# Two fill products between a step's row scores and its key scores: a fused attention and Fourier kernel on one Trainium2 core

## The chip, the cores and the metric

The kernel runs on one core of a Trainium2 chip. The core has five engines with their own queues: TensorE for matrix products (PE; PEld is its loading of the stationary operand), VectorE (DVE), ScalarE (ACT), GpSimd (POOL) and SyncE (SP), whose queue issues almost all DMAs. The metric is the time of one execution in microseconds, measured on the device. Three executions of the kernel before took 2702.86, 2702.91 and 2704.59 us (median 2702.91).

## The reference

Two independent layers are computed in float32, and their results are laid side by side:

```python
# A: attention, 32 heads of width 32 that share one key head and one value head; S = 2048, D = 1024
q = (x @ wq).reshape(B, S, H, Dh).transpose(0, 2, 1, 3)
k = x @ wk
v = x @ wv
p = softmax(einsum("bhqd,bkd->bhqk", q, k) * Dh ** -0.5)
a = einsum("bhqk,bkd->bhqd", p, v).transpose(0, 2, 1, 3).reshape(B, S, D) @ wo
# B: real part of a two-dimensional Fourier transform as matrix products
y = dft_seq_re @ (x @ dft_hid_re.T) - dft_seq_im @ (x @ dft_hid_im.T)
out = concatenate([a, y], axis=-1)
```

## The kernel before

**Products.** Each float32 product of 128x512 is made of three products of split operands (`rh`, `rl` of the right side, `mh`, `ml` of the left side, a high and a low part each), and they accumulate in one of two PSUM banks named `psb`. These products, for the query projection, the Fourier layer and the output projection, are called **fill products** here. They stand in one long list of groups of 12 or 24 products. `take(n)` issues the next n of them and, when a group ends, its copy or addition out of `psb` on DVE; `pump` issues the loads and splits that later products need.

**Attention.** The attention runs as a loop of 1024 steps, 32 units of 32 steps. A unit is 512 query rows of four heads. In step n the loop issues, in this order on PE:

- a pair of products into a `pss` tile: scores with the query rows on the partitions, 128 rows by 1024 keys (`scores`). DVE takes the row maximum into `nm` (TENSOR_REDUCE), and ACT later forms exp(score - maximum) and its row sum (ACTIVATE and ACTIVATION_READ_ACCUMULATOR on `pss`). These are the **row scores**, and they run 44 steps ahead of the key scores. `score_step(s)` issues the pair of score s, then on ACT the row sum of score s-1. There are two `pss` tiles, so the pair of score s waits for the row sum of score s-2.
- a pair of products into the `pst` tile: scores with the keys on the partitions, 128 keys by 1024 query columns, with the log of the row's sum already folded in (`expo`). ACT turns them into probabilities `p`. These are the **key scores**. There is only one `pst` tile, so the pair of step n waits for the exponential of step n-1.
- at three steps of each unit (r = 0, 12 and 22, `ENDS`), called **block ends** here: a block of products of `p` with the values `v` (`pv`), which may first finish a few fill products (`aside`).
- at every other step: some fill products, `level(n)`. It spreads the remaining list evenly up to the next block end, and comes out at 4 to 7 a step. The step ahead of a block end holds five fill products at 91 of the 95 block ends that have a block of values (6 or 7 at the others), by the program's own order.

At r = 16 `inverse` issues four DMAs that fetch the inverse row sums (`rb`). In the last 44 steps no row scores are left, and a step is a key-score pair and six or seven fill products.

All engines keep the order in which the program was written (`keep_in_program_order`), so an instruction that waits on PE holds up everything behind it there. Every instruction stands under line 79 in the profile, the one that keeps this order, so groups are told apart by tile.

Of the kernel before, what the change touches and what calls it, by code (L numbers as in the profile page):

```python
# [101 lines left out]
def tile_kernel(ctx: ExitStack, tc, xT, wq, wkv, wo, xbT, wT, cT, out):  # L102
# [51 lines left out]
    class Line:  # L154
# [24 lines left out]
        def pump(self):  # L179
            for k in range(4):  # L180
                while self.may(k) and self.items[self.n[k]].due - self.lead[k] <= pos["fill"]:
                    self.step(k)
# [94 lines left out]
    def add(gs):  # L277

        for g in gs:
            i0 = g.at = end[0]  # L280
            end[0] += g.n
            if groups and g.set[0] is not groups[-1].set[0]:
                prev["set"] = prev["this"]
                prev["this"] = i0
            for c, it in enumerate(g.right):
                if it.need is None:
                    it.need = i0 + 3 * c
                    p0 = min(prev["set"], i0 - it.back)
                    it.due = min(it.need, p0 + (i0 - p0) * (g.first + c + 1) // (len(g.set) * len(g.right))) - it.ahead
                    RL.items.append(it)  # L290
                it.last = i0 + 3 * c + 2
            for c, it in enumerate(g.left):
                if it.need is None:
                    it.need = it.due = i0 + 12 * c
                    ML.items.append(it)
                it.last = i0 + 12 * c + 11
            for it in g.ys:
                it.due = i0 + g.n
                ylist.append(it)
            groups.append(g)  # L300
# [14 lines left out]
    def at(p, f):  # L315
        k = len(later)
        while k and later[k - 1][0] > p:
            k -= 1
        later.insert(k, (p, f))

    def run_later():
        while later and later[0][0] <= pos["fill"]:
            later.pop(0)[1]()
# [29 lines left out]
    def bank(name, open_=False):  # L353

        while held:
            held.pop(0)()
        b = 1 - cur["bank"] if cur["bank"] is not None else int(used[1] < used[0])
        cur["at"] += 1
        used[b] = cur["at"]
        if open_:  # L360
            cur["bank"] = b
        return ps_b[b].tile([P, W], F32, name=name)
# [10 lines left out]
    def product(g, ps, j):  # L373
        c, w = divmod(j, 3)
        l, r = g.left[c // 4], g.right[c]
        a = (l.lo if w == 2 else l.hi)[:, c % 4]
        te.matmul(ps[:g.rows], a, r.lo if w == 1 else r.hi, start=j == 0, stop=j == g.n - 1)

    def take(n):
        for _ in range(n):  # L380
            if cur["group"] >= len(groups):
                return
            g = groups[cur["group"]]
            j = pos["fill"] - g.at
            if j == 0:
                cur["ps"] = bank("psb", True)
            if j % 3 == 0:
                RL.force(g.right[j // 3])
            if j % 12 == 0:
                ML.force(g.left[j // 12])  # L390
            product(g, cur["ps"], j)
            pos["fill"] += 1
            if j == g.n - 1:
                cur["group"] += 1
                assert all(hasattr(it, "done") for it in g.ys)
                g.post(cur["ps"])
                cur["at"] += 1
                used[cur["bank"]] = cur["at"]
                cur["bank"] = None
                if g.ys:  # L400
                    at(pos["fill"] + 2 * BEHIND + 5, lambda n=len(g.ys): yused.__setitem__(0, yused[0] + n))
            pump()
            run_later()
# [174 lines left out]
    def wo_set(e):  # L578
        return [Item([(lambda g=g: wo[g * P:(g + 1) * P, e * W:(e + 1) * W], 1)]) for g in range(NG)]
# [90 lines left out]
    def o_group(b, t, e, ws):  # L670
        def post(ps):
            r0 = b * W + t * P
            to = out[r0:r0 + P, e * W:(e + 1) * W]
            if b < NQ - 1:
                oo = op.tile([P, W], F32, name="qh")
                dve.tensor_copy(oo, ps)
                store(to, oo)
                return

            n = len(halves)  # L680
            halves.append(n)
            oo = pp.tile([P, 2, W], F32, name="p")
            if n + 1 < 8:
                if n % 2:
                    dve.tensor_copy(oo[:, 0], ps)
                else:
                    act.activation(oo[:, 0], ps, AF.Copy)
                move(act, to, oo[:, 0])
                return
            for k, q in enumerate((act, sp)):  # L690
                cols = slice(k * W // 2, (k + 1) * W // 2)
                if k:
                    dve.tensor_copy(oo[:, k, :W // 2], ps[:, cols])
                else:
                    act.activation(oo[:, k, :W // 2], ps[:, cols], AF.Copy)
                move(q, to[:, cols], oo[:, k, :W // 2])
        return Group([o_left(b, t, q) for q in range(2)], ws, post)
# [101 lines left out]
    def inverse(u):  # L799
        rb[u] = onp.tile([P, W], F32, name="rb")  # L800
        for h in range(4):
            r = r_d[u][4 * h:4 * h + 4].rearrange("t c -> (t c)")
            sp.dma_start(rb[u][h * DH:(h + 1) * DH], r.unsqueeze(0).to_broadcast([DH, W]))

    def expo(n):
        u, r = divmod(n, SU)
        c, hp_ = divmod(r, 2)
        pt[u, c, hp_] = pp.tile([P, 2, W], F32, name="p")
        ps = ps_t.tile([P, 2, W], F32, name="pst")
        for a in range(2):  # L810
            te.matmul(ps[:, a], kst[:, c * P:(c + 1) * P], qst[u][:, 2 * hp_ + a], start=True, stop=True)
        act.activation(pt[u, c, hp_], ps, AF.Exp)
# [45 lines left out]
    def score_step(s):  # L858

        if s < total:  # L860
            u, r = divmod(s, SU)
            if r == SU - 6 and u + 1 < len(units):
                open_unit(u + 1)
        if SU <= s < SU * (len(units) + 1) and s % SU == TURN:
            row_sums(s - 1)
            lse_3((s - SU) // SU)
        if s < total:
            scores(s)
        row_sums(s - 1)
        u, e = divmod(s - SU, SU)  # L870
        if 0 <= u < len(units):
            for f in LSE.get(e, ()):
                f(u)
# [52 lines left out]
    def goal(n):  # L926
        return PRO + (FILL - PRO - LAST - MORE * (total - QUIET)) * n // total + MORE * max(n - QUIET, 0)
# [4 lines left out]
    def level(n):  # L932
        r = n % SU
        if r in ENDS:
            return
        more = min(e for e in ENDS if e > r) - r
        left = goal(n + more) - pos["fill"]
        take(round(left / more))

    for n in range(total):  # L940
        u, r = divmod(n, SU)
        if n == total - 12:
            w1 = wo_set(1)
            add([o_group(NQ - 1, t, e, ws) for e, ws in ((0, w0), (1, w1)) for t in range(4)])
        score_step(n + SU + LEAD)
        if ends:
            ends.pop(0)()
        expo(n)
        if r == 16:
            inverse(u)  # L950
        if r in ENDS and n:
            pv((n - 1) // SU, (ENDS.index(r) - 1) % (len(CUT) - 1))
        level(n)


    last = groups[len(groups) - 8:]
# [75 lines left out]
```

## Time and profile before

| what | value |
|---|---|
| median of three executions | 2702.91 us |
| profiled execution's own time | 2701.05 us |
| its span, first to last instruction | 2699.3 us |
| ACT busy | 2134.8 us (79%) |
| POOL busy | 1723.7 us (64%) |
| DVE busy | 1592.8 us (59%) |
| row maximum on DVE (TENSOR_REDUCE `nm<-pss`) | 1024 of 1223 ns |
| exponential of the row sums on ACT (`pss<-pss,nm`) | 1024 of 1089 ns, and 207 ns to read the sum |
| exponential of the key scores on ACT (`p<-pst`) | 1030 ns each |

All times below come from one execution, whose own time is 1.9 us under the median. Matmuls overlap: one that is listed with 0.39 us starts about 0.23 us after the one before, and its listed end is modelled. So how fast PE goes is read from where matmuls start, and a wait of PE shows as idle time ahead of a load of weights (PEld), which is the instruction that carries the wait.

### The profile page before, as it was taken

What the parts mean: (1) busy time and instruction counts of PE and PEld (TensorE: products, weight loads), DVE (VectorE), ACT (ScalarE), POOL (GpSimd) and SP (SyncE); (2) the same over time, 40 slices, a digit from 0 to 9 for tenths busy, and PEclk for the clock granted to TensorE, in tenths of its full rate; (3) what the DMA queues carried; (4) which work ended last, traced back from release to release, by engine and by line L of the source; (5) the groups of instructions that cost most, each with busy time, mean ns of one, the idle gap of its engine ahead of it and who ended that gap; (6) DMA issues with size and microseconds to landing.
All of it is one profiled execution on the core that took longest, in us unless ns stands there. A gap on an engine that the chain in (4) does not pass through costs nothing.

```text
span 2699.3 us, 40577 instructions
## 1 busy us (share of the span) xinstructions
PE 2691.8 (100%) x13820; PEld 1918.1 (71%) x13820; DVE 1592.8 (59%) x1826; ACT 2134.8 (79%) x3131; POOL 1723.7 (64%) x1711
## 2 busy tenths in 40 slices
PE   9999999999999999999999999999999999999999
PEld 6876767676777767677776777667677776767767
DVE  5766666666666666565565656666565555655411
ACT  3588888888888888888888888888888888888741
POOL 4854425777547558765556675576887987865751
PEclk9999999999999999999999999999999999999999
DMA  8543336887788566564354588984675765644665
GB/s 277 190 136 128 114 97 202 282 285 233 241 268 281 203 226 195 175 193 142 125 160 152 183 258 278 306 262 128 213 226 161 223 199 159 209 142 134 192 211 187
DMA packets 316931, 538.24 MB, mean 199 GB/s; under 512 B 35962, under 2 KB 63354, under 8 KB 316666
## 3 DMA queue, kind: packets, MB, share of 16 engines
q1 hardware_dynamic: 315572, 533.69, 61.6%
q8 instruction: 109, 1.79, 0.3%
q10 hardware_dynamic: 1152, 1.97, 0.2%
q14 instruction: 98, 0.80, 0.1%
HBM read 395.58 MB, written 138.15 MB: 198 GB/s over the span
## 4 chain that ended last, share of the span: by engine, by line
PE 99%; ACT 0%; DVE 0%; DMA 0%; SPq 0%; issue 0%; ACTq 0%
PE psb L79 62%; PE pss L79 19%; PE pst L79 18%; ACT pss L79 0%; DVE nm L79 0%; DMA p<-in_xT_dram 0%; ACT p L79 0%; SPq L79 0%; DVE y L79 0%; DVE qh L79 0%; DVE rl L79 0%; ACT rh L79 0%; DVE p L79 0%; ACTq L79 0%
## 5 line engine op out<-in xcount | busy, mean ns | idle before, releaser
L79 DVE TENSOR_REDUCE nm<-pss 128x1 f32<-128x1024 f32 x1024 | 1252.5, 1223 | 562.0 <-PE pss L79 561.3
L79 ACT ACTIVATE p<-pst 128x1024 f32<-128x1024 f32 x1026 | 1056.6, 1030 | 437.7 <-PE pst L79 425.1
L79 ACT ACTIVATE pss<-pss,nm 128x1024 f32<-128x1024 f32 x1024 | 1114.7, 1089 | 57.2 <-DVE nm L79 55.5
L79 PE MATMUL psb<-rh,mh 128*128 128x512 f32 x1790 | 698.2, 390 | 0.3 <-ACT rh L79 0.3
L79 PE MATMUL psb<-rl,mh 128*128 128x512 f32 x1790 | 697.8, 390 | 0.6 <-DVE rl L79 0.5
L79 PE MATMUL psb<-rh,ml 128*128 128x512 f32 x1790 | 697.7, 390 | 0.0
L79 PE MATMUL pss<-kst,qst 128*128 128x512 f32 x2048 | 641.5, 394 | 0.2
L79 PE MATMUL pst<-qst,kst 128*128 128x512 f32 x2048 | 641.0, 394 | 0.5 <-ACT p L79 0.3
L79 POOL TENSOR_TENSOR ml<-m,mh 128x512 fp32r<-128x512 f32 x366 | 473.5, 1294 | 35.1 <-ACT mh L79 26.2
L79 PEld LDWEIGHTS pss<-kst,qst 128*128 128x128 f32 x2048 | 377.9, 188 | 125.4 <-issue 51.1
L79 PE MATMUL psb<-p,v 128*32 128x512 f32 x4096 | 459.3, 594 | 0.0
L79 PEld LDWEIGHTS pst<-qst,kst 128*128 128x128 f32 x2048 | 375.0, 188 | 103.0 <-ACT p L79 27.0
L79 PEld LDWEIGHTS psb<-rh,mh 128*128 128x128 f32 x1790 | 336.0, 188 | 75.6 <-ACT rh L79 1.8
L79 PEld LDWEIGHTS psb<-rl,mh 128*128 128x128 f32 x1790 | 336.0, 188 | 73.7 <-DVE rl L79 1.9
L79 PEld LDWEIGHTS psb<-rh,ml 128*128 128x128 f32 x1790 | 336.0, 188 | 71.1
L79 POOL CAST mh<-m 128x512 fp32r<-128x512 f32 x365 | 224.5, 615 | 229.1 <-PE psb L79 211.9
L79 PEld LDWEIGHTS psb<-p,v 128*32 128x32 f32 x4096 | 123.3, 110 | 283.0 <-issue 275.2
L79 POOL TENSOR_TENSOR m<-m,m 128x512 f32<-128x512 f32 x220 | 284.4, 1293 | 54.5 <-DMA m<-o 19.6
L79 POOL TENSOR_TENSOR rl<-r,rh 128x512 fp32r<-128x512 f32 x208 | 269.2, 1295 | 4.0
L79 POOL CAST rh<-r 128x512 fp32r<-128x512 f32 x208 | 129.0, 620 | 194.2 <-PE psb L79 147.3
L79 ACT ACTIVATION_READ_ACCUMULATOR pss<-pss,nm 128x1 f32 x1024 | 212.5, 207 | 0.0
L79 POOL TENSOR_TENSOR r<-r,r 128x512 f32<-128x512 f32 x120 | 155.1, 1293 | 52.3 <-DMA r<-in_wT_dram 33.6
(92 smaller groups left out, 791.3 us busy)
## 6 DMA issues: line engine op xcount, KB each, us to landing
m<-in_cT_dram SPq DMA_DIRECT2D x384, 256.0 KB
r<-s SPq DMA_DIRECT2D x192, 256.0 KB
y<-y SPq DMA_DIRECT2D x128, 256.0 KB
r<-in_wT_dram SPq DMA_DIRECT2D x88, 256.0 KB
m<-in_xbT_dram SPq DMA_DIRECT2D x88, 256.0 KB
y<-u SPq DMA_DIRECT2D x80, 256.0 KB
m<-in_wq_dram SPq DMA_DIRECT2D x64, 256.0 KB
qst<-qh SPq DMA_DIRECT2D x64, 256.0 KB
```

Of the source, the lines that this page charges most:

```text
L79: return lambda *a, **k: self.tc.keep_in_program_order(f(*a, **k))
```

## The change

In a step, the first two of the fill products now come between the row-score pair and the key-score pair; the others stay behind both. `level` returns the number instead of issuing the products. It returns 0 at a block end, and there the key-score pair still follows the row-score pair at once.

```diff
     def level(n):
         r = n % SU
         if r in ENDS:
-            return
+            return 0
         more = min(e for e in ENDS if e > r) - r
         left = goal(n + more) - pos["fill"]
-        take(round(left / more))
+        return max(round(left / more), 0)
...
         score_step(n + SU + LEAD)
         if ends:
             ends.pop(0)()
+        fill = level(n)
+        first = min(fill, 2)
+        take(first)
         expo(n)
         if r == 16:
             inverse(u)
         if r in ENDS and n:
             pv((n - 1) // SU, (ENDS.index(r) - 1) % (len(CUT) - 1))
-        level(n)
+        take(fill - first)
```

The order of instructions on PE at an ordinary step, near the end of unit 16 (`pss` row scores, `pst` key scores, `psb` fill products), before:

```order
L79 MATMUL pss<-kst,qst_758 128x512 x2
L79 MATMUL pst<-qst_1386,kst 128x512 x2
L79 MATMUL psb<-rh,mh 128x512
L79 MATMUL psb<-rl,mh 128x512
L79 MATMUL psb<-rh,ml 128x512
L79 MATMUL psb<-rh,mh 128x512
L79 MATMUL psb<-rl,mh 128x512
L79 MATMUL pss<-kst,qst_758 128x512 x2
L79 MATMUL pst<-qst_1386,kst 128x512 x2
```

And the same place with the change:

```order
L79 MATMUL pss<-kst,qst_758 128x512 x2
L79 MATMUL psb<-rh,mh 128x512
L79 MATMUL psb<-rl,mh 128x512
L79 MATMUL pst<-qst_1386,kst 128x512 x2
L79 MATMUL psb<-rh,ml 128x512
L79 MATMUL psb<-rh,mh 128x512
L79 MATMUL psb<-rl,mh 128x512
L79 MATMUL pss<-kst,qst_758 128x512 x2
L79 MATMUL psb<-rh,ml 128x512
L79 MATMUL psb<-rh,mh 128x512
L79 MATMUL pst<-qst_1386,kst 128x512 x2
```

The key-score pair moved behind two fill products in both steps, so from pair to pair there are still nine products. The next place on PE is the block end right behind, where unit 17 begins: the last step of unit 16, the row and key scores of the block end, and the block of values (`psb<-p,v`). Before:

```order
L79 MATMUL pss<-kst,qst_758 128x512 x2
L79 MATMUL pst<-qst_1386,kst 128x512 x2
L79 MATMUL psb<-rh,ml 128x512
L79 MATMUL psb<-rh,mh 128x512
L79 MATMUL psb<-rl,mh 128x512
L79 MATMUL psb<-rh,ml 128x512
L79 MATMUL psb<-rh,mh 128x512
L79 MATMUL pss<-kst,qst_758 128x512 x2
L79 MATMUL pst<-qst_2057,kst 128x512 x2
L79 MATMUL psb<-p,v 32x512 x20
```

With the change:

```order
L79 MATMUL pss<-kst,qst_758 128x512 x2
L79 MATMUL psb<-rh,ml 128x512
L79 MATMUL psb<-rh,mh 128x512
L79 MATMUL pst<-qst_1386,kst 128x512 x2
L79 MATMUL psb<-rl,mh 128x512
L79 MATMUL psb<-rh,ml 128x512
L79 MATMUL psb<-rh,mh 128x512
L79 MATMUL pss<-kst,qst_758 128x512 x2
L79 MATMUL pst<-qst_2057,kst 128x512 x2
L79 MATMUL psb<-p,v 32x512 x20
```

Here only the first of the two key-score pairs moved: from its start to the start of the next pair there were nine products, and there are seven now. The other engines' orders stay as they were, but for the SP queue: in seven of the 32 units the fetch of `rb` at r = 16 now stands behind the one to four DMAs that the two fill products issue. One of these places, as the difference of the two orders (`u` and `y` are Fourier sums, whose buffer only has another number; `w` and `qh` are parts of the output weights):

```order
-L79 DMA u_0_1_264<-y_6478 128x512
-L79 DMA rb<-r_205 32x512 x4
+L79 DMA u_0_1_264<-y_6473 128x512
 L79 DMA w_2_1_145<-qh 128x512
 L79 DMA w_2_1_146<-qh 128x512
+L79 DMA rb<-r_205 32x512 x4
```

The fetch moved behind two stores; what it fetches is read 16 steps later.

## The prediction

> **What bounds the kernel now.** I read the page first, its first part, its slices and its chain.
>
> ```profile
> PE 2691.8 (100%) x13820; PEld 1918.1 (71%) x13820; DVE 1592.8 (59%) x1826; ACT 2134.8 (79%) x3131; POOL 1723.7 (64%) x1711
> ...
> PEclk9999999999999999999999999999999999999999
> ...
> PE 99%; ACT 0%; DVE 0%; DMA 0%; SPq 0%; issue 0%; ACTq 0%
> ```
>
> PE is busy nearly all the time, at full clock, and 99% of the chain that ended last is PE. The change adds and removes no instruction, so time can only come from or go into stops of PE. The list of waits of PEld, the loads of weights, tells where it stops now (microseconds, times, longest).
>
> ```profile
> PEld pst L79 <- ACT p L79: 27.0, 108, 0.7
> ...
> PEld pss L79 <- ACT pss L79: 0.8, 2, 0.5
> ```
>
> Key-score pairs wait 108 times for ACT to free the one `pst` tile; row-score pairs almost never wait. What a wait costs is read in the timeline, at two stops in a row (start, length, engine, what, idle time before).
>
> ```profile
> 338.05 1.03 ACT L79 ACTIVATE p<-pst 128x1024 f32<-128x1024 f32 x1
> ...
> 338.76 0.61 PE L79 MATMUL pss<-kst,qst 128*128 128x512 f32 x2
> 338.97 1.08 ACT L79 ACTIVATE pss<-pss,nm 128x1024 f32<-128x1024 f32 x1
> 339.13 0.30 PEld L79 LDWEIGHTS pst<-qst,kst 128*128 128x128 f32 x2 [0.18 <-ACT p L79]
> 339.21 0.65 PE L79 MATMUL pst<-qst,kst 128*128 128x512 f32 x2
> ...
> 339.70 0.39 PE L79 MATMUL psb<-rh,ml 128*128 128x512 f32 x1
> ...
> 342.05 1.04 ACT L79 ACTIVATE p<-pst 128x1024 f32<-128x1024 f32 x1
> ...
> 342.70 0.61 PE L79 MATMUL pss<-kst,qst 128*128 128x512 f32 x2
> ...
> 343.15 0.30 PEld L79 LDWEIGHTS pst<-qst,kst 128*128 128x128 f32 x2 [0.26 <-ACT p L79]
> 343.15 0.74 PE L79 MATMUL pst<-qst,kst 128*128 128x512 f32 x2
> ...
> 343.73 0.40 PE L79 MATMUL psb<-rh,ml 128*128 128x512 f32 x1
> ...
> 344.05 0.26 ACT L79 ACTIVATE nm<-nm 128x32 f32<-128x32 f32 x1
> 344.17 1.06 ACT L79 ACTIVATE p<-pst 128x1024 f32<-128x1024 f32 x1
> ```
>
> At the first stop the exponential ends at 338.05 + 1.03 = 339.08, the load starts 0.05 later, and the second product of the pair starts one spacing (0.23) ahead of the fill product at 339.70, at 339.47: 0.39 after the exponential's end. Without the wait, four products from the row pair at 338.76 on would have brought that fill product at 338.76 + 4 x 0.23 = 339.67, so the stop cost 0.03 where the list says 0.18. At the second stop the same sum gives 343.73 - 342.70 - 0.91 = 0.12 where the list says 0.26. So a wait costs its listed idle time less 0.15 (the load is otherwise early by that much), and the 108 waits cost 27.0 - 108 x 0.15 = **10.8 us**. That is all that moving the key scores could win. The law that I carry on: the second product of a key pair starts no sooner than 0.39 after the end of the exponential before it.
>
> **The change part by part.** The place that decides is a block end, here the last step of unit 16 and the first of unit 17.
>
> ```profile
> 1469.13 0.62 PE L79 MATMUL pss<-kst,qst 128*128 128x512 f32 x2
> ...
> 1469.59 0.62 PE L79 MATMUL pst<-qst,kst 128*128 128x512 f32 x2
> ...
> 1469.89 0.20 ACT L79 ACTIVATION_READ_ACCUMULATOR pss<-pss,nm 128x1 f32 x1
> 1470.04 0.39 PE L79 MATMUL psb<-rh,ml 128*128 128x512 f32 x1
> ...
> 1470.24 1.03 ACT L79 ACTIVATE p<-pst 128x1024 f32<-128x1024 f32 x1
> ...
> 1470.95 0.39 PE L79 MATMUL psb<-rh,mh 128*128 128x512 f32 x1
> ...
> 1471.16 1.08 ACT L79 ACTIVATE pss<-pss,nm 128x1024 f32<-128x1024 f32 x1
> 1471.17 0.62 PE L79 MATMUL pss<-kst,qst 128*128 128x512 f32 x2
> ...
> 1471.63 0.61 PE L79 MATMUL pst<-qst,kst 128*128 128x512 f32 x2
> ...
> 1472.16 0.20 ACT L79 ACTIVATION_READ_ACCUMULATOR pss<-pss,nm 128x1 f32 x1
> 1472.17 0.64 PE L79 MATMUL psb<-p,v 128*32 128x512 f32 x4
> ```
>
> Products start 0.2275 apart (1470.04 to 1470.95 is four of them). The exponential starts 0.65 after its pair (1469.59 to 1470.24) and ends at 1471.27. ACT had been free since 1470.09, so it is the pair that sets it. The next pair's second product stands at 1471.63 + 0.23 = 1471.86 and is allowed from 1471.27 + 0.39 = 1471.66: slack 0.20, in a step of five fill products.
>
> *An ordinary step.* The key pair goes 0.455 later and its exponential with it, and so does the next pair: there are nine products from pair to pair before and after. The slack of 0.20 is what it was. No gain in the steady run, then. What the move does give is room ahead of the exponential: ACT works off the row sum of score s-1 and then the exponential, and a row sum that is late because DVE's maximum is late now has 0.455 more before it makes a pair late. Of the 10.8 us I let 7.3 go and 3.5 stay. What stays are the steps that are short in themselves: the stop at 339.13 follows a step of four fill products, eight from pair to pair, and cost 0.03; by the program's order there are 49 such steps, 1.5 us. And the steps without row scores near the end, where six fill products and a pair make eight as well; the chain of waits in order of time shows them.
>
> ```profile
> 2576.41 1.38 PE psb L79 x6
> 2577.79 0.52 PE pst L79 x2
> ```
>
> 1.38 + 0.52 = 1.90 for eight products, where 8 x 0.2275 is 1.82: 0.08 each, some 25 of them by the program's order, 2.0 us. Bounds: none or all of the 10.8 goes.
>
> *A block end.* `level` gives 0 there, so the block end's key pair is not moved, while the pair of the step ahead is, and its exponential with it, by 0.455. Slack 0.20 becomes a stop of 0.455 - 0.20 = **0.255**, and nothing hides it: the block of values, the next row pair and everything after stand behind it on PE. Pair to pair are seven products, 1.59, where 0.65 + 1.03 + 0.39 - 0.23 = 1.84 is needed. There are 3 x 32 block ends less the one at n = 0: 95 x 0.255 = 24.2 us. One of them, in unit 30, follows a step without row scores that has no slack, so it pays the whole 0.455: +0.2. The step behind a block end has its pair 0.455 later than now, but is not short of time, so nothing comes back.
>
> *A late ACT at a block end.* Where the exponential ahead of the end isn't set by its pair but by ACT, the stop differs. The row at 344.17 is the step ahead of r = 22 in unit 2: a small exponential of 0.26 (344.05) stands ahead, and the key exponential starts 0.25 after it could. That ACT work is in one step of each unit, so this is between nothing and 32 x 0.25 = 8 us. I take 2, since in units with longer steps ACT has caught up by then.
>
> *Row scores.* The row sum of score s-2 comes behind the exponential on ACT, so it moves 0.455 too, while the pair of score s that needs its tile does not. The row sum that starts at 1471.16 has its sum read by 1472.16 + 0.20 = 1472.36, and by the same law a second product could follow at 1472.75. In a run of five-product steps (nine products, 2.05) the pair that needs this tile has its second product at 1471.17 + 2.05 + 0.23 = 1473.45: 0.70 to spare, 0.245 after the change. A step of four takes another 0.23 off and comes to nothing. So waits of row pairs, 0.8 us now, may come in those 49 steps. Bounds: nothing, or as much as key pairs lose today, 10.8. I take 2, nearer to the row of today.
>
> *The queues.* In seven units SP's fetch of `rb` goes behind up to four other DMAs; it is read 16 steps (over 30 us) later: nothing. DVE, ACT and POOL keep their order.
>
> Sum on the profiled execution's own 2701.05 us (its span of 2699.3 and 1.75 around it): - 10.8 + 3.5 + 24.2 + 0.2 + 2 + 2 = +21.1, **2722 us**. The median of the runs lies 1.9 us over this execution, which the range covers.
>
> **The rivals.** *Row pairs stop too.* With 0.245 to spare in a five-product step and none in a four-product one, any lateness of ACT lands on `pss`. For it: ACT needs 1470.24 to 1471.16, then 1.12 to the next exponential at 1472.28, 2.04 a step, as much as PE takes. Against: exponentials that follow their pair leave ACT no lateness. At today's cost of the key pairs, 10.8 instead of 2: 2731.
>
> *A shorter stop.* If the weights of the waiting pair were already in the array, the second product would follow 0.05 + 0.23 = 0.28 after the exponential instead of 0.39, and each block end would cost 0.11 less, 10.4 us in all: 2712. Against it: both stops quoted load only after ACT's end, at 339.13 and 343.15. The Trainium skill, page "TensorE: Matmul & The Clock Gate", section "Step-by-step: what each phase is for", says that the engine pulls a load of weights ahead of products in flight into a background buffer. By that rule it would come out this way; the two rows say that it does not reach past a wait.
>
> *No change.* The stops at the block ends and the waits that go are about the same. That needs ends of about 7.3 / 95 = 0.08 us, a third of what the rows give, and 5.4 us (0.2%, about what a measurement of this kernel can tell from no change) to either side count as this. For it: ends that have more slack than the one quoted. Against: 91 of 95 follow a step of five products.
>
> *Faster.* If at the block ends the exponential were set by ACT's queue, not by its pair, a pair that comes 0.455 later would not move it; the block ends would stay as they are and the 7.3 would be won: 2694. It decides from an exponential that starts 0.455 or more after its pair would allow. For it: ACT needs 2.04 us a step. Against: at 1470.24 ACT had been free for 0.15, and the late one at 344.17 is late by 0.25 only.
>
> **How the numbers follow.** Forecast 0.67, row pairs too 0.16, shorter stop 0.07, no change 0.06, faster 0.04. The forecast's own bounds are 2701 + 24.4 - 10.8 = 2715 with no lateness at all and 2733 with the 8 us of late ends and half the waits kept. The range reaches from 2713 to 2733, which takes in the row pairs' case and leaves out the last three, 0.17. Slower 0.90, same 0.06, faster 0.04.
>
> **What would show it.** Right: the waits of PEld on `pst` for ACT rise from 108 to some 150 or more and from 27.0 to over 50 us, and most stand right behind a row pair at r = 0, 12 and 22, with an idle time of 0.25 + 0.15 = 0.40 each; the exponential still starts 0.65 after its pair. Wrong: block ends with a listed wait under 0.3, fewer than 90 of them, waits of PEld on `pss` of more than 5 us, or as many waits at ordinary steps as today.

## The result, and the profile after

The changed kernel takes **2725.84 us** (median of five, 2725.13 to 2726.22), against 2702.86 us (median of five, 2702.47 to 2704.59): a ratio of 1.0085, 95% interval 1.0074 to 1.0096. The forecast was 2722, in a range of 2713 to 2733. The profiled execution's span is 2724.1 us, 24.8 more than before; the medians lie 23.0 apart, because the profiled execution of the kernel before was 1.8 us faster than its median. The page after, the lines that answer to those shown of before (busy time of each engine, and the shares of the chain that ended last):

```profile
PE 2713.4 (100%) x13820; PEld 1911.3 (70%) x13820; DVE 1593.2 (58%) x1826; ACT 2129.7 (78%) x3131; POOL 1722.5 (63%) x1711
...
PE 85%; ACT 9%; issue 3%; DMA 1%; DVE 1%; POOL 1%; SPq 0%; DVEq 0%; POOLq 0%; ACTq 0%
```

The number of products is the same, ACT and POOL are busy for less time than before and DVE for 0.4 us more, and the chain now runs through ACT for 9% of the span. A busy PE of 100% hides the stops, since the listed ends of matmuls (0.39 after the start, where the next one starts after 0.23) bridge short ones. The waits of PEld, the loads of weights, show them (microseconds, times, longest):

```profile
PEld pst L79 <- ACT p L79: 58.4, 170, 0.9
PEld pss L79 <- ACT pss L79: 6.9, 26, 0.5
```

With 0.15 us taken off each wait, as in the prediction, key pairs lose 58.4 - 170 x 0.15 = 32.9 us (10.8 before) and row pairs 6.9 - 26 x 0.15 = 3.0 us (0.5 before). Together that is 24.6 us more, of the 24.8 that the span grew between these two executions. The same block end as in the prediction, in the timeline of the kernel after:

```profile
1482.56 0.62 PE L79 MATMUL pst<-qst,kst 128*128 128x512 f32 x2
...
1482.86 0.20 ACT L79 ACTIVATION_READ_ACCUMULATOR pss<-pss,nm 128x1 f32 x1
...
1483.21 1.03 ACT L79 ACTIVATE p<-pst 128x1024 f32<-128x1024 f32 x1
...
1484.29 0.30 PEld L79 LDWEIGHTS pst<-qst,kst 128*128 128x128 f32 x2 [0.41 <-ACT p L79]
1484.29 0.73 PE L79 MATMUL pst<-qst,kst 128*128 128x512 f32 x2
```

The exponential starts 0.65 after its pair (1482.56 to 1483.21), as before, and ends at 1484.24. The load of the block end's key pair starts 0.05 later, with 0.41 of idle time listed: 0.41 - 0.15 = 0.26 us lost, where the prediction had 0.255. ACT had read the row sum by 1483.06, so the pair set the start of the exponential here.

Not all block ends are like this one. I added up over the whole trace how much later than one spacing the two products of each block end's key pair start: 29.8 us at the 95 of them. Most (61) lose 0.25 or 0.26. Those with a step of four fill products two steps ahead lose 0.38 to 0.41 at r = 0 and 12, and 0.48 to 0.53 at r = 22. One of the last kind, in unit 5:

```profile
581.35 1.04 ACT L79 ACTIVATE p<-pst 128x1024 f32<-128x1024 f32 x1
...
582.56 0.62 PE L79 MATMUL pst<-qst,kst 128*128 128x512 f32 x2
...
583.25 0.23 ACT L79 ACTIVATION_READ_ACCUMULATOR pss<-pss,nm 128x1 f32 x1
...
583.35 0.26 ACT L79 ACTIVATE nm<-nm 128x32 f32<-128x32 f32 x1
583.47 1.06 ACT L79 ACTIVATE p<-pst 128x1024 f32<-128x1024 f32 x1
...
584.57 0.30 PEld L79 LDWEIGHTS pst<-qst,kst 128*128 128x128 f32 x2 [0.66 <-ACT p L79]
```

Here the exponential could have started at 582.56 + 0.65 = 583.21, but ACT was still reading the row sum, which ended at 583.48, and had the small exponential in between: it starts at 583.47, 0.26 late, and the block end loses 0.66 - 0.15 = 0.51.

### The profile page after: what moved, and what is told of

Read it like the earlier page. It is cut to its first block, busy times and chain, and to the rows that moved or that the text cites. A ratio compares the mean times of both kernels' runs of the same rounds, so it can differ in the third digit from the quotient of the medians.

```text
span 2724.1 us, 40577 instructions
## 1 busy us (share of the span) xinstructions
PE 2713.4 (100%) x13820; PEld 1911.3 (70%) x13820; DVE 1593.2 (58%) x1826; ACT 2129.7 (78%) x3131; POOL 1722.5 (63%) x1711
## 4 chain that ended last, share of the span: by engine, by line
PE 85%; ACT 9%; issue 3%; DMA 1%; DVE 1%; POOL 1%; SPq 0%; DVEq 0%; POOLq 0%; ACTq 0%
PE psb L79 54%; PE pss L79 16%; PE pst L79 16%; ACT pss L79 6%; ACT p L79 2%; DVE y L79 1%; DMA y<-c 0%; DMA w<-qh 0%; DMA qh<-in_wo_dram 0%; DMA m<-in_xbT_dram 0%; DVE qh L79 0%; SPq L79 0%; DVE nm L79 0%; POOL m L79 0%; DMA c<-y 0%
## 5 line engine op out<-in xcount | busy, mean ns | idle before, releaser
L79 PEld LDWEIGHTS pst<-qst,kst 128*128 128x128 f32 x2048 | 371.1, 188 | 126.8 <-ACT p L79 58.4
```

The source lines that it names most:

```text
L79: return lambda *a, **k: self.tc.keep_in_program_order(f(*a, **k))
```

## The experiments

Three theories were put against each other. **L**: at each place it counts whether the distance from key pair to key pair covers pair, exponential and restart (1.84 us). **B**: what counts is how many products stand in the stretch between two block ends, because ACT needs some 2.03 us a step there (2.04 in the prediction's rows, 2.01 in those of the second experiment), about as much as the 2.05 of nine products that PE gives it. **Q**: it costs something at every step that products with other weights stand between the score pairs. The diffs are against the changed kernel. The runs are counted in their order: the fifth kernel is that of "Two products moved within the stretch".

**Only the step ahead of a block end.**

```diff
-        first = min(fill, 2)
+        first = min(fill, 2) if r + 1 in ENDS else 0
```

> Only the step ahead of a block end has its key pair moved behind two fill products; every other step is as before the change. Theory L (at a block end the exponential of the pair ahead isn't done: seven products from pair to pair, 1.59 us, where 1.84 are needed): the block ends cost what they cost with the whole change, 95 x 0.255 = 24 us or a little more, and none of the 10.8 us of old stops goes: 2727 us (2724 to 2732). Theory B (the loss is that two products leave the stretch between two block ends, in which ACT has as much to do as PE): here no product leaves the stretch, since the pairs behind a block end stay, so the time is that of before within 5 us. Rival Q (the cost is that products with other weights now stand between the score pairs, at every step): 1 of 10 steps changed, a tenth of the loss, 2705.

Measured: 2721.53 us, ratio 1.0071 (1.0056 to 1.0086). With one key pair moved in ten to twelve steps, most of the loss is there, so Q falls, and so does B as the only cause, for the stretch lost nothing. The same block end in its timeline:

```profile
1480.37 0.62 PE L79 MATMUL pst<-qst,kst 128*128 128x512 f32 x2
...
1481.02 1.02 ACT L79 ACTIVATE p<-pst 128x1024 f32<-128x1024 f32 x1 [0.60 <-PE pst L79]
...
1482.10 0.30 PEld L79 LDWEIGHTS pst<-qst,kst 128*128 128x128 f32 x2 [0.40 <-ACT p L79]
```

ACT waited 0.60 for the pair, so it wasn't short of time, and the block end still loses 0.25. Summed over the block ends the loss is 25.1 us, nearly all of them at 0.25: with ACT rested, the late ones are gone. The time is 2.5 us below the range that L gave. I had expected all 10.8 us of old stops to stay; by the list of waits (56.1 us in 164 waits, 31.5 us of loss) 6.4 stay.

**Drawn down ahead of the block end.**

```diff
-        first = min(fill, 2)
+        first = min(fill, 2, min(e for e in ENDS if e > r) - r - 1)
```

> The change, but the two products between the pairs are drawn down ahead of a block end: two, then one in the last step but one, none in the last. No pair-to-pair distance falls by more than one product. L alone (each distance for itself: eight products are 0.03 us short): two such steps for each block end, 0.06 x 95 = 6 us, and the old stops stay gone: 2702 (2699 to 2707). B (ACT needs 2.03 us a step in the stretch and the stretch is two products shorter, wherever these are taken): the stop of about 0.25 us only comes one step earlier: 2722 (2716 to 2728). Q: as the whole change, 2726.

Measured: 2718.3 us, ratio 1.0059 (1.0044 to 1.0074): within B's range, far from L's. The two steps that are one product short, in unit 5 (r = 9, 10 and 11):

```profile
552.25 0.61 PE L79 MATMUL pst<-qst,kst 128*128 128x512 f32 x2
...
552.90 1.03 ACT L79 ACTIVATE p<-pst 128x1024 f32<-128x1024 f32 x1
...
553.98 0.30 PEld L79 LDWEIGHTS pst<-qst,kst 128*128 128x128 f32 x2 [0.18 <-ACT p L79]
...
554.91 1.03 ACT L79 ACTIVATE p<-pst 128x1024 f32<-128x1024 f32 x1
...
555.99 0.30 PEld L79 LDWEIGHTS pst<-qst,kst 128*128 128x128 f32 x2 [0.33 <-ACT p L79]
```

The first short step costs 0.03, as L says. But the exponential behind it starts 2.01 after the one before, which is all ACT can do with a row sum in between, so the second costs 0.18. One short step uses up the slack; two in a row pay.

**Fill products at the block ends too.**

```diff
         first = min(fill, 2)
+        if r in ENDS:
+            take(2)
```

> The change, and at the block ends too two fill products come between the two score pairs; they are taken from the steps in between, so some 90 more steps have four fill products instead of five or six. Pair to pair is nine products at the block ends again. L alone: the stops at the block ends go (-29.8 us of the 32.4 us that key pairs lose now), and 90 short steps cost 0.03 us each: 2699 (2696 to 2704). B: the products that the short steps lack are missing against ACT's 2.03 us a step, some 0.2 us each: 2714 (2708 to 2720). Q: 2726 or more.

Measured: 2711.91 us, ratio 1.0037 (1.0023 to 1.0051): B's range again. Key pairs lose only 5.4 us (30.8 us in 169 waits), so the block ends are cured. But row pairs lose 9.5 us (22.9 us in 89 waits): nearly all of them stand behind a step of four fill products, and the products that the block ends took made such steps more frequent. These waits account for 3.6 of the 10.7 us that the profiled span grew over the kernel before. Three blocks of values that wait 0.6 to 0.7 for DVE (at 504.00, for instance) add 1.9; where the rest lies is open.

**The key pair inside the block of values.** At a block end two chunks of the block come first, then the key pair, then the rest of the block.

```diff
+        block = iter(())
+        if r in ENDS and n:
+            block = pv((n - 1) // SU, (ENDS.index(r) - 1) % (len(CUT) - 1), 2)
+            next(block)
         expo(n)
...
-        if r in ENDS and n:
-            pv((n - 1) // SU, (ENDS.index(r) - 1) % (len(CUT) - 1))
+        for _ in block:
+            pass
```

> The change, but at a block end the key pair stands behind the first two fifths or so of the block of values (two of its five or six key chunks, about 0.84 us), which need only older probabilities. Pair to pair into the block end becomes seven products and 0.84 us, 2.43 us, more than 1.84 needed and more than ACT's 2.03. L and B alike: the stops at the block ends vanish, key pairs keep only their 2.6 us elsewhere, row pairs their 2.1 us: 2725.8 - 29.8 = 2696 (2693 to 2700), faster than both kernels. Q (products between the pairs cost by themselves) or a cost at the row pairs: still over 2710.

Measured: 2729.26 us, ratio 1.0099 (1.0084 to 1.0114). That was wrong by 33 us. Its waits of key pairs for the exponential, and its block end:

```profile
PEld pst L79 <- ACT p L79: 14.2, 75, 0.4
```

```profile
1485.59 1.92 PE L79 MATMUL psb<-p,v 128*32 128x512 f32 x16
...
1487.44 0.30 PEld L79 LDWEIGHTS pst<-qst,kst 128*128 128x128 f32 x2 [0.84 <-ACT pss L79]
1487.44 0.73 PE L79 MATMUL pst<-qst,kst 128*128 128x512 f32 x2
1488.11 2.78 PE L79 MATMUL psb<-p,v 128*32 128x512 f32 x24
```

The stops went as forecast: 14.2 - 75 x 0.15 = 3.0 us of the 32.9 are left. But the kernel became 3.4 us slower instead of 29.9 faster, so each of the 95 interruptions of a block costs (29.9 + 3.4) / 95 = 0.35 us. The rows show where: the pair takes 0.67 from its start to the next product (1487.44 to 1488.11), not 0.455, and the trace has 0.52 from the last narrow product to the pair, where the next four narrow ones would have come after 0.41. That is 0.21 and 0.11, 0.32 together. The pair waited for nothing: the 0.84 of idle time is listed under ACT's row sum, but that was read by 1486.68, and the same idle time of the load is put down to "issue" at 53 of the 95 interruptions. Going from the narrow 128x32 products to full ones costs the same 0.52 at the end of a block in the kernel before; here this passage and the one back are paid once more.

**Two products moved within the stretch.** The step behind a block end keeps its pairs together and gives two products to the step ahead of the next one. From key pair to key pair every distance is that of the kernel before.

```diff
         left = goal(n + more) - pos["fill"]
-        return max(round(left / more), 0)
+        if r - 1 in ENDS:
+            return max(round(left / more) - 2, 0)
+        return max(round((left - 2 * (more > 1)) / more), 0)
...
-        first = min(fill, 2)
+        first = 0 if r - 1 in ENDS else min(fill, 2)
```

> The change, with two products moved within each stretch: the step behind a block end has two fill products fewer and both its pairs together, as before the change, and the step ahead of a block end has two more. From key pair to key pair the distances are those of the kernel before, at every place (nine products into 93 of the 95 block ends); only the row pairs stand two products earlier. L and B alike: no distance fell and no product leaves the stretch, so no stop at the block ends comes in, and the room that row sums won stays: of the old 10.8 us of key pairs' stops some 3 stay, and 2 us at the row pairs: 2701 - 7.8 + 2.1 = 2696 (2693 to 2700), faster than both kernels. Q (products between the pairs cost by themselves): more than 2715. If the 8 us of old stops went for another reason than the room ahead of the exponential: 2701 to 2705.

Measured: 2697.26 us (median of 11, 2696.77 to 2699.09), ratio to the kernel before 0.9981 (0.9972 to 0.9990). It is faster than both kernels, and Q is out: nine of ten steps have products between their pairs. The same block end, and its waits:

```profile
1466.61 0.61 PE L79 MATMUL pst<-qst,kst 128*128 128x512 f32 x2
...
1467.26 1.03 ACT L79 ACTIVATE p<-pst 128x1024 f32<-128x1024 f32 x1
...
1468.42 0.41 PEld L79 LDWEIGHTS pst<-qst,kst 128*128 128x128 f32 x2
1468.65 0.61 PE L79 MATMUL pst<-qst,kst 128*128 128x512 f32 x2
```

```profile
PEld pst L79 <- ACT p L79: 16.7, 83, 0.7
PEld pss L79 <- ACT pss L79: 6.9, 26, 0.5
```

The exponential ends at 1468.29, and the next load at 1468.42 doesn't wait. Key pairs lose 16.7 - 83 x 0.15 = 4.2 us and row pairs 3.0: 4.1 less than before, as the span has it (2695.2 against 2699.3). So the room ahead of the exponential takes 6.6 of the 10.8 us of key-pair stops away, where the prediction had 7.3, when it isn't paid for at the block ends.

**One and three products between the pairs.** `min(fill, 1)` and `min(fill, 3)` in place of `min(fill, 2)`.

> One fill product between the pairs instead of two. L: the distance into a block end is eight products, 1.82 us, of 1.84 needed: 0.03 us at each, and the late ones (a short step or the small exponential ahead) add some 5 us as with two; of the old stops at ordinary steps more stay than with two, 3 to 5 us; row pairs 1 us: 2704 (2701 to 2709). Q: half of the loss, 2714.

> Three fill products between the pairs. L: the distance into a block end is six products, 0.48 us short: 95 x 0.48 = 46 us and some 5 us of late ones; key pairs elsewhere 2.6 us. Row pairs have 0.24 - 0.23 = 0.01 us to spare in a step of five and none in one of four, so they lose 5 to 12 us: 2701 - 10.8 + 51 + 2.6 + 8 = 2752 (2746 to 2762). Q: one and a half times the loss, 2737.

Measured: 2705.75 us, ratio 1.0011 (1.0001 to 1.0020), and 2757.1 us, ratio 1.0201 (1.0187 to 1.0215). Both lie in L's ranges and not at Q's numbers. One product costs 3 us, two 23, three 54: not in proportion, because the first uses up a slack of 0.20 us. At most block ends the key pair is late by 0.03 us with one, 0.26 with two and 0.46 to 0.49 with three.

**The shares of the steps rounded down.**

```diff
-        return max(round(left / more), 0)
+        return max(left // more, 0)
```

> The change with the share of each step rounded down, so that steps of four products stand early in a stretch and the step ahead of a block end takes the rest: the distance into a block end is eight products at 54 of the 95 block ends and seven at 40. The sum over the stretch is the same. L alone: 54 x 0.03 + 41 x 0.255 = 12 us at the block ends, no lateness from short steps right ahead of them: 2709 (2705 to 2713). B: what the block ends don't lose is lost at the short steps early in the stretch, 2720 or more.

Measured: 2712.83 us, ratio 1.0037 (1.0023 to 1.0051). This is inside L's range, at its upper edge, and well below B's. So the count of products in a stretch doesn't set the loss by itself; it matters how short steps (of four fill products) follow each other. Where two of them stand together behind a block end, as in unit 5, the row pair pays:

```profile
568.42 0.30 PEld L79 LDWEIGHTS pss<-kst,qst 128*128 128x128 f32 x2 [0.33 <-ACT pss L79]
```

That is 0.18 us. Where the distance into a block end is eight products, one short of nine, most ends (50 of 54) lose 0.03. L with one addition fits the stops read in these kernels: a distance that is one product short costs only 0.03 while ACT isn't late already, and ACT recovers only where a step takes longer than the 2.01 to 2.04 us that ACT needs.

**The work on the row sums three steps later.**

```diff
-    TURN = 3
-    LSE = {0: (lse_1,), 1: (lse_1b,), 2: (lse_2,), 5: (lse_4,)}
+    TURN = 6
+    LSE = {3: (lse_1,), 4: (lse_1b,), 5: (lse_2,), 8: (lse_4,)}
```

> The change, with the work on a unit's row sums (DVE's small reductions and ACT's small exponential of 0.26 us, which stands in the step ahead of r = 22) three steps later, behind that block end. If the stops at r = 22 are larger than at the other ends because of this exponential (10.8 us at r = 22, against 9.0 and 9.9 at r = 0 and 12), they fall to 0.26 us each, and to 0.4 where a step of four products stands two steps ahead: some 9.3 us, 1.5 us less, 2724 us (2723 to 2726). If a step of four products ahead is the cause alone, r = 22 stays at 10.8 us and the time at 2726.

> The fifth kernel (distances of the kernel before, row pairs two products earlier) with the same later work on the row sums. Key pairs lose 0.7 us at r = 22 and some 0.6 us in the steps ahead of it there, row pairs 0.8 us: up to 1.5 us less, 2696 us (2694 to 2698). If the small exponential only comes late elsewhere: 2697 to 2698.

Measured: 2775.1 us, ratio 1.0267 (1.0253 to 1.0281), and on the fifth kernel 2747.18 us, ratio 1.0164 (1.0150 to 1.0178). The part that was asked came as expected: in the first of the two the stops at r = 22 fall from 10.8 to 9.5 us in all, 0.25 each and 0.38 to 0.40 behind a step of four. But both times were expected to fall by up to 2 us, and some 49 us of something else came in. In the first kernel:

```profile
PEld pss L79 <- ACT p L79: 33.6, 30, 1.4
PEld pss L79 <- DVE mt L79: 14.4, 25, 0.6
```

The move also took the transposition of the row sums, which uses a `pss` tile and waits for DVE, out of the place right behind a block of values, where the block covers its waits. That this is the cause is argued from the list and from the program; the two runs below leave the transposition in its place and don't have this loss. I had not counted what else the two numbers move.

**Only the small exponential one step later, at the block end.**

```diff
-    LSE = {0: (lse_1,), 1: (lse_1b,), 2: (lse_2,), 5: (lse_4,)}
+    LSE = {0: (lse_1,), 2: (lse_1b, lse_2), 5: (lse_4,)}
```

> The change, with only ACT's small exponential of the row sums one step later, at the block end r = 22 itself, behind that step's row sum; its transposition stays behind the block of values, which covers it. The stops at r = 22 come to what they were in the ninth kernel, 9.5 us against 10.8, and nothing new comes in: 1.3 us less on key pairs, 2724.5 us (2723.5 to 2725.5). If DVE, which then waits for the small exponential at the block end, is late for what follows: 2727 or more.

> The fifth kernel with the small exponential at the block end r = 22 too: key pairs lose 0.7 us less at r = 22, row pairs a little less: 2696.5 us (2695.5 to 2697.3), against 2697.3. If DVE is late behind it: 2698 to 2701.

Measured: 2725.02 us, ratio 1.0084 (1.0070 to 1.0098), and on the fifth kernel 2697.22 us, ratio 0.9979 (0.9970 to 0.9988). The stops at r = 22 come to 9.7 us against 10.8, as expected, so the small exponential is one cause of the lateness there. In the time neither kernel can be told from the one without this edit.

## Why the prediction was right, and where its sizes were off

- *10.8 us is all that can be won, by taking 0.15 off each listed wait.* Right: with the same rule the waits after give 24.6 of the span's 24.8 us.
- *Ordinary steps: no gain in the steady run, 7.3 of the 10.8 us go with the room ahead of the exponential.* Right: key pairs lose 32.9 - 29.8 = 3.1 us outside the block ends, where 3.5 were forecast. By the starts of products the steps near the end have 2.1 us of it (2.0 forecast), but only 21 steps of four cost a key pair its 0.03, 0.6 us in all, and not 49 (1.5 forecast). The fifth experiment, without the loss at the block ends, has 4.2 us of key-pair stops left and is 5.5 us faster than the kernel before.
- *Block ends: 95 x 0.255 = 24.2 us.* Right: most stops measure 0.26, and the first experiment, with hardly any lateness, 25.1 us in all. The one in unit 30 lost 0.70 where it had lost 0.23 before, so it paid the whole 0.455 as forecast.
- *A late ACT at block ends: 2 us.* This term was mis-sized: 29.8 - 24.4 = 5.4 us. The prediction named only the small exponential ahead of r = 22, in one step of a unit. What I didn't see is that a step of four fill products two steps ahead of any block end makes ACT late too, by 0.12 to 0.15 us; there are 25 such ends. The small exponential accounts for only 1.1 us, by what the run that moved it alone took off at r = 22. The bound of 8 us held the sum, though not for the reason that the prediction gave for it.
- *Row pairs: 2 us.* 3.0 by the rule, 0.5 of it from before the change, so the size was near, and the place was right: 24 of the 26 waits stand behind a step of four. The listed 6.9 us are over the 5 that I had named as a sign against the forecast. The rival that row pairs cost as much as key pairs didn't come.
- *The rival of a shorter stop* is out: the load comes 0.05 after the exponential's end and the loss is 0.26 at the end shown, not 0.145. The Trainium skill's rule that loads of weights are pulled ahead (page "TensorE: Matmul & The Clock Gate", section "Step-by-step: what each phase is for") did not help here: in the rows shown these loads, which carry the wait themselves, start only after the exponential has ended.
- *The queues: nothing.* The waits after list the fetch of `rb` at r = 16 once, for 0.6 us of DVE, and never for PE. No run tested SP's moved fetch by itself.

In all the forecast of +21.1 us fell 3.7 short of the profiled span's +24.8, mostly by the late ends (3.4).

## What to carry to other kernels

A stage that moves later at most steps, but not at every one, shortens the distance at each border between moved and unmoved steps; work out that one distance against the round trip (here pair, exponential and restart, 1.84 us) before the steady steps, which don't change at all. Where two engines need the same time a step, as PE and ACT do here, slack is spent once: the first short step cost 0.03 us and the next one 0.18. The cure was to leave those distances as they were, by moving two products from behind one border to ahead of the next, and not to break into a block of other products.

## What the runs showed of the hardware

A key pair in the middle of a block of narrow 128x32 products cost 0.35 us more for each interruption (95 of them, 33.3 us in all), though it waited for nothing. Waits cost PE less here than their listed idle time: 0.15 us of each was no loss, at stops from 0.03 to 0.5 us. In all the kernels but the one that splits the block, this rule gives the loss of key pairs within 1 us of what the starts of the products give.
